# A hand-planned order of 3311 steps, planned anew for the attention part, with eight cross-engine waits in place of ten

## The chip, the core and the metric

The kernel runs on one core of a Trainium2 chip. Five engines work side by side, each through its own instructions in the order in which they were issued: TensorE (PE), VectorE (DVE), ScalarE (ACT), GpSimd (POOL) and SyncE (SP), which only starts DMAs here. The metric is the device time of one execution in microseconds.

## The reference

A local causal attention with a memory term, then two mixture-style feed-forward blocks one after the other on the same tokens:

```python
scores = (q @ k.T) / sqrt(64), causal          # 4 batches, 8 heads, 576 tokens, 64 wide
local = softmax(scores) @ v
q_p = phi(q)                                   # phi(x) = x + 1 for x > 0, else exp(x)
mem_out = (q_p @ M_prev) / (q_p . z_prev + 1e-6)
x = g * mem_out + (1 - g) * local              # g = sigmoid(beta) of the head
x = x as 2304 tokens x 512
x = mish(x @ w_in) @ w_out                     # 512 -> 2048 -> 512
x = silu(x @ w2_in) @ w2_out                   # 512 -> 2048 -> 512
```

## The kernel before

**Steps.** The kernel does not schedule itself. It registers 3311 named steps (`Steps.add`), each a Python function that issues one or a few instructions of one engine, and `Steps.issue` calls them in the order of a table, `ORDER`, which is a base64 string of step numbers. The tile library then puts semaphores where tiles are shared. So the table fixes the order on every engine's queue, that of the DMA issues on SP among them, and also which of a ring's buffers a step gets.

**The attention** works on 16 pairs of heads, numbered 0 to 15; a step is written "pair.step" below. ld.. loads qT, kT, nq and nv (L353). phu, phe (ACT, L385, L386), phn, phf, phz, phy (POOL, L388 to L394) and phr (DVE) make phi(q) and its product with z. The scores s0 to s41 are PE matmuls (L473, L508); r.. (DVE, L466) scale them, mask them and take the row minimum; e.. (ACT, L491) are the exponentials. zd, phq, zg, phmh, phml, phm0 are the scale factors and the scaled phi (DVE and POOL). X1, X2, X3 and W are transposes on PE (L366) that are copied out of PSUM by ACT and DVE (L356, L359; the step names end in Ah and Bh). Rw and Rl send the row scales through DRAM and back into a tile R (L448, L453, L455). Vhi and Vlo are the products with v (L565), and Vhic and Vloc (DVE, L569) multiply them by R and write the tokens into xT.

**The feed-forward blocks** (the MoE part) run 24 visits, each a group of four weight blocks on a third of the tokens. A product Q:vc/n (visit v, half c, product n, L881 to L883) is six matmuls into PSUM; s1, s6, s5 (ACT, L910) copy partial sums out, c11, c22, c21 (DVE, L908) add to them, m.. (ACT) are the activation functions, and h0, l0, h1, l1 split the result in a high and a low part (ACT L919, DVE L920). O:vc/.. are the six-matmul pieces of the second matrix (L948). The tokens are split once per third (0, 1, 2) by casts h.. (ACT, L853) and subtractions T.. and l.. (DVE, L846); sp.. (SP, L860) spills such a tile to DRAM. Weights are decoded in steps W:job/ld, abs, b0, b1, b2, b3 (DVE, L687 to L702) and hi (ACT, L723), lo (POOL L728 for the first four jobs, DVE for the others), and combined in steps C (L747).

**The manual waits.** `AFTER` is a list of pairs of step numbers: the second step's first POOL instruction waits for the first step's last DVE instruction, which is always a weight decoding step.

```python
for first, second in AFTER:
    if n == second:
        one, two = (next(i for i in x if i.engine == e) for x, e in (
            (reversed(of[first]), tc.nc.vector.engine), (of[second], tc.nc.gpsimd.engine)))
        tc.add_manual_dep(two, one.name, ...reason="no port shared")
```

Of the kernel before, what the change touches and what calls it, by code (L numbers as in the profile page):

```python
# [1130 lines left out]
ORDER = (
    "BQAGAEMABwBEAC4AKQBCABcAKgAAAAEAKwACAC8ALAADAIAAMAAcABoABAAYAG8KGwAdAB8ACQASAEYACwAKAAgAEQAtAEcADABIABMAgQAZABUA"
    "ZgANABQAawBZAB4AaQAOAGcASQAWAL4AbAAPAFQAIABaAGgASwBwChAAagB/ADEAXABbAEoAJAAyAFcAbQCDACEAVQC9ADQAWAAzAHEKNQBOACMA"
    "JQAmAEUANwBMACIATwA2AFYAhQA9AF0AvABSADgAPgBQAJYAhAA/APkAqABTAIYAowCZAFEAlwCpADsAOgCRAHUKqgCIAKYAhwCYAKQAXgCUADkA"
    "wACSAGEATQClAG4Acgo8AIsAbwBiAGAAcQCMAJoAcwBjACcAlQA2AXQAjwCnAHIAjQDCAHAA+wCJAMEAdQBfAHMKwwDOAHYAdwCOAPoA4AAoAHoA"
    "0QCQAEAAxAB8AHsAzwCTAHgAigB0CuUAxQDSAIIA0wCrAEEA0ACbAOYA4wBkAOEAOAGcAKwAdgquAC8M1gCxANQA/QCtAJ0AsADXAHkAtwDGAK8A"
    "5wDVAMgA/wB1AbkA/gDJALIAuADKAMcA5AAAAbUAzABzAbMACwHiALQAzQAQAXcKAgE3AQwBngA6AQEBfQBlAKAADgHLALYAEwF4Cp8AIgHoAB0B"
    "FAF+AL8AoQDpAHkKPAHrAA0BHgHqABEB7gB7Cg8BIwEgAe0AAwEkAfQA7AAhAQUBBAH2APUABgEfAaIA7wA7AbABCQHYAPAAPQHxAE0B2QAHAboA"
    "dAEKAVABPwEIAU4BegryANsAsgFRAbsASAF3AXwK3QAwDFoBeQESAV8BSwH3AE8BJQFgAfMAXQHcAFsBPgFJAUwBsQEYAdoAXAFDARoBJgF9CkIB"
    "KAFhAUAB7wFKATIM3gBGAV4BKwG0AUQBKQGBCkcBKgH4AJwBJwHfABkBMQyXAUUBMQGaAZgBFQEyATMBQQHuATMMhQF4ARcBFgEsAZ0BegFiAYgB"  # L1140
    "LwGeAfwAigGGAZkBUgEtAWMBiwFlAYcBfAGNAWYBVAGbAYABZwEwAVMBLgF/AXsBjgFVAYMBiQFpAYEBVgFkAcIBLAK2AX4KfQHUAWoB2QGEAYIK"
    "GwF+AcUBKwJoAYwB1wE0DMMBggFrATUMOQHEAccB1QGfATYMHAHxAW4BoAFXAcYB7QGiATQB2gGkAcoBbwHIAaMBOAxwAaUBkgHWAYMKoQG8AbUB"
    "bAEqAjUBOgy9AdsBlAGrAcABkwHLAbcBZwK+AY8BwQERAq0BFgLJAf8BkQG4AW0B2AEUAqwBFwKmARICdgG5AQICGAIEAvMBvwG6AVgBAwIHAqkB"
    "aQIFArsBpwHcAYQK8gEAAi4CcQGFCggC3QGqAYYK3wEGAvoBqAGQAd4BhwrgAfkBcgEBAlkB4QHPATAC/QGVAeIB0AH0AdEBNwz7AbMBFQJ/Ci8C"
    "9QHjAf4BEwKWAWgCQQLkAeUBTgJEAlMC9gFCAugBMQL8AaYCVAJPAjwC6gHpAVECQwLMATICGQL3AUUCrgHmAaQCPwLNAfgBPQI8DDMCUAIJAhoC"
    "pQKvAWsCHAIbAs4BNwIfAgoCNgJtAgsCQALwAQwCOgJVAiUCDQI0Ah4CPgJ5AucBHQInAjsC6wE5DDgCJgJ6AjkCIwLjAjUCfAKLAiACUgKICoAK"
    "fgIOAnsCiQqQAlYC0gF9AowCJAJXAoECWQIhAlgCjgJaAqgCfwKPCpECXAIiAmwCdAJbAqoC7AFiAm4C0wGSAnMCZAJjAkYCggJ3AnACYAJJAuEC"
    "jQJvAkgCSgK7AngCdQJdAj4MLQJLAqkCtgK+Aj8MRwJxAigCvwJhArwCcgJ2AqsCuQLiAo8CzQK3AsgCugIpAg8CrAJeAl8CIAOAAssCyQK9Aq0C"
    "zgKKCsoCkwKQCrACHgM7DIsKhgLMApQCsQIQArgClgJMApgCagK0AogClwKHArIC5QKZAq4CQAwfA+YC+AJNApUCtQLnAvMC+wJdA7MC+QKfAvYC"
    "rwLPAj0MmgKgAqECBQP8AtACCgP0Ap0CZQJbA/oC0QIIA9ICmwIGA9MCjArWAgcDgwILA40KZgLUAu4CnAKeAoQC6ALtAoUCCQPDAgwDpwLvAtwC"  # L1150
    "xAKRCukCNQPdAt4C9wKiAjYD2gJcAyIDOAPqAvEC1QIkA0cDQQzFAkIDIwOjAtcC9QKSCiUDMAPbAtkC2ALrAsACOQOaA4kCkwpCDMEC8gJDAzMD"
    "lwrwAuwCMQMmA98CRAOKAl8DRQMNAw4DNANIA8ICDwMAA+QCJwNEDBADKgPgAhMDKAMCAysDRgw3AxkDLAMBA8YCGgMbAxEDLQOUChIDFwOZA0YD"
    "LgMyA4QDKQOYCmEDfwNgA8cCmAP9AoIDLwOAAxQD/wJJA20DYgOFAxgDgwMWAxUDcgNKA24D/gKfCjoDmQqcA2QDAwNLA3UDYwOGA3ADbwNzA54D"
    "mgohA00DZQNxA0wDaANQAzsDPANnA08DQwwEA1YDTgNpA3YDZgNRA50DRQxrA6oDgQNYA1IDrwOfA1MDVwMcA6sDdANUA60DagOhA6ADsgPBA2wD"
    "XgOwA7wDHQM9A7EDmwpZA64DwgNVAz8DswO/A4cDvQN3Az4DnArAA6QDiAO+A6IDpwqlA4oDwwONA0ADrAOoA44KeAOmA6kDWgOJA4wDpwN5A5MD"
    "mwOjA0EDiwPEA5QDlQN6A8UDfAOgCo4DkQPHA3sDxgPKA5ADjwO0A8gD0AO1A7YDyQPRA9IDywPVA6gKFwR9A84DzQOSA8wDGAQdBBMEGgS3A88D"
    "0wOhCrgDFAS5A5YDJgSpCh4EIAS6AxsEFQQcBNQDoQQjBCcEtQQkBKgElQqqCqIEfgOWCigEuwOXA6MEqwTWAyEEMASkBK8EqwqpBLgEFgS8BBkE"
    "MQQpBLYEMgSsCqUEvwQ0BCoEtwSqBDMEKwSmBL0ErQTDBCwErQq5BKwEogotBLEEpwS+BKMKrwo7BOIErgSkCrAEugQ8BLMEJQThBMEEnQq0BMAE"
    "5ASeCrIE6ARIBLsE6wT1BCIEwgQ1BMQE9gQuBMcEyQSwCjkESQTMBB8EpQo6BEUEpgr4BMgExQTPBO8ExgTjBC8EtwpGBNAE6QT8BDYEygT/BD4E"
    "NwTNBEsEOATLBPcETATRBM4EsQrSBP0EQQTVBEIEPQTlBLgKuQq6CtgE6gS7CrIK2QSzCrwK5gRDBL0K+QTsBD8EVATWBLQKUQTtBMMK/gTTBLUK"  # L1160
    "AQUDBVIE+gTXBPEEvgrbBFMEtgpVBNwErgrECucE3QS/Ck4E3gRABO4EAAXACvAETwQkBdQE8gQhBUQEIgVWBCgF8wT7BAUF9AQjBVcExQrGCtoE"
    "AgXfBFAExwoEBVgEOAXgBAcFwQoJBSkFyAoIBTUFyQoGBSUFPAU3BSoFLQUmBT0FJwXKCssKOQXMCkcMwgosBSsFDAVIDM8KSgwvBUkMPgUPBUsM"
    "TAwQBUoETQxODGEFQQVQDDEFNgUyBToFPwVoBc0KOwUNBVMMQgXOChEFCgVSDFQM1woOBVYMEgVVDAsFVwzQChMFLgVYDDAFFQVZDEMFWgzRClsM"
    "YgUYBdIKXAxPDGMFMwVRDNMK2AoWBdQK2QrfCmQF2goXBTQFFAUbBWsFaQVdDEQFWQQeBWUF4AocBeEKagVHBeIKHwVABUgFHQV2BUUF4wpvBdsK"
    "GQXkCkYFZgXnChoFIAVeDEkF3Ap4BXUF7wPoCkwFfAV/BXcFbQXpCk8F6gp9BU0EbAVKBWcFSwV5BUcETQV+BXEFgQVSBesKTgVuBXoFcgVwBeAD"
    "7Ap7BYAFcwWhBYIFUwXXA1UFVAWoBVgFWQXvClAFWgVbBd0DVgWjBVcFgwWEBV4F+wOkBdUKhQXWCqIFXwWrBYYFrwXsA7UF3Qp0BakFXAWHBfAK"
    "UQXxCqUF8grtCogFYAXaA4kFqgXeCrwF7gqMBfMKpgX0CrcF9QqNBb0FrAW4BbEF+wpdBbkF5QrhBb4F8APBBbYFsgX2CroF6AWtBb8FjwX3CuED"
    "+Ar8CooF+QqOBZAF+gr9CqcFiwUBC+MFrgWwBbsFswWSBfwDtAWVBeYK6QXABcIF4gX+Cv8K5QUCC+QF6gWWBe0FAAvnBQMLBwvrBeYF7wXuBQQL"
# [137 lines left out]
```

## Time and profile before

| what | value |
|---|---|
| median of three runs | 924.39 us (923.96 to 924.99) |
| the profiled execution | 924.26 us, of which the span from the first to the last instruction is 922.5 |
| mean granted TensorE clock | 0.996 of full speed |
| busy share of the span | PE 99%, DVE 69%, ACT 50%, POOL 13% |
| attention on PE | from 4.81 us to about 159.9 us |
| first product of the feed-forward part on PE | 159.91 us |

The busy shares are averages over two stages: up to about 160 us the attention, in which DVE and ACT are as full as PE, and after that the feed-forward blocks, in which PE alone is full.

### The profile page before, as it was taken

The page shows a single profiled execution, that of the slowest core. Times are in us where ns is not written, and L with a number is a line of the kernel's source. Part 1 is how long each engine was busy: PE and PEld are TensorE (multiplying, and loading weights), DVE is VectorE, ACT ScalarE, POOL GpSimd, SP SyncE. Part 2 cuts the span into 40 slices and gives each one's busy share as a digit, 9 for nine tenths or more (in the row PEclk, how much of TensorE's full clock was granted, in tenths as well). Part 3 has the DMA queues.
Part 4 walks back from the last instruction along what each step waited for, and adds up shares of the span by engine and source line. Part 5 has one row for each costly group of instructions (what it writes and reads, how often), then busy time and mean ns, then how long its engine had stood idle before and what let it go on. Part 6 is the DMA issues. An engine that isn't in the chain of part 4 may idle for free.

```text
span 922.5 us, 15456 instructions
## 1 busy us (share of the span) xinstructions
...
## 2 busy tenths in 40 slices
...
GB/s 243 197 220 209 198 201 117 260 225 121 134 307 148 89 79 176 206 47 125 142 173 64 148 194 126 129 170 214 169 140 47 192 200 88 1 102 199 20 58 171
DMA packets 54794, 139.50 MB, mean 151 GB/s; under 512 B 7216, under 2 KB 26816, under 8 KB 54720
## 3 DMA queue, kind: packets, MB, share of 16 engines
...
q14 instruction: 27, 0.22, 0.1%
...
## 4 chain that ended last, share of the span: by engine, by line
PE 90%; DVE 3%; ACT 3%; DMA 1%; issue 1%; SPq 1%; POOL 0%; ACTq 0%; DVEq 0%; POOLq 0%
PE acc L948 44%; PE psX L881 7%; PE psX L883 7%; PE psX L882 7%; PE psY L881 4%; PE psY L883 4%; PE psY L882 4%; PE ps_t L565 3%; PE ps_s L473 3%; PE ps_t L366 2%; PE psW L883 2%; PE psW L881 2%; PE psW L882 2%; DVE sm L466 1%; ACT Ph L491 1%
## 5 line engine op out<-in xcount | busy, mean ns | idle before, releaser
L948 PE MATMUL acc<-g,w 128*128 128x384 f32 x1152 | 217.6, 338 | 0.0
L948 PE MATMUL acc<-w,g 128*128 128x512 f32 (+1 forms) x876 | 213.6, 392 | 0.0
L948 PEld LDWEIGHTS acc<-g,w 128*128 128x128 f32 x1152 | 203.9, 188 | 0.2 <-DVE g L920 0.2
L948 PEld LDWEIGHTS acc<-w,g 128*128 128x128 f32 x876 | 162.2, 188 | 31.7
L910 ACT COPY vt<-psX 128x384 f32<-128x384 f32 x144 | 67.8, 479 | 189.0 <-PE psX L883 158.3
L973 DVE TENSOR_TENSOR xT<-acc,xT 128x384 f32<-128x384 f32 (+2 forms) x127 | 75.8, 607 | 83.3 <-PE acc L948 83.2
L920 DVE TENSOR_TENSOR g<-vt,g 128x768 fp32r<-128x768 f32 x96 | 91.7, 965 | 37.8 <-ACT g L919 37.7
L908 DVE TENSOR_TENSOR vt<-psY,vt 128x384 f32<-128x384 f32 x96 | 52.8, 554 | 70.7 <-ACT vt L910 41.3
L919 ACT CAST g<-vt 128x768 fp32r<-128x768 f32 x96 | 78.7, 834 | 26.4 <-PE acc L948 25.5
L466 DVE CUSTOM_DVE_ANT_0 sm<-ps_s,mask 128x448 f32<-128x448 f32 (+3 forms) x128 | 66.6, 551 | 11.4 <-PE ps_s L473 7.5
L916 ACT ACTIVATE vt<-vt 128x768 f32<-128x768 f32 x48 | 40.3, 845 | 54.9 <-DVE vt L908 54.7
L881 PE MATMUL psX<-x,w 128*128 128x384 f32 x192 | 64.9, 338 | 0.4 <-ACT vt L910 0.4
L473 PE MATMUL ps_s<-kT,qT 64*128 64x288 f32 (+3 forms) x320 | 61.2, 474 | 3.7 <-DVE m L466 3.3
L881 PE MATMUL psY<-xT,w 128*128 128x384 f32 x192 | 64.7, 337 | 0.0
L883 PE MATMUL psY<-xT,w 128*128 128x384 f32 x192 | 64.7, 337 | 0.0
L883 PE MATMUL psX<-x,w 128*128 128x384 f32 x192 | 64.7, 337 | 0.0
L882 PE MATMUL psY<-xT,w 128*128 128x384 f32 x192 | 64.7, 337 | 0.0
L882 PE MATMUL psX<-x,w 128*128 128x384 f32 x192 | 64.7, 337 | 0.0
L756 ACT CAST w<-val 128x512 fp32r<-128x512 f32 (+1 forms) x64 | 35.3, 566 | 44.6 <-DVE val L747 20.7
L747 DVE TENSOR_TENSOR w<-val,w 128x512 fp32r<-128x512 f32 (+1 forms) x56 | 34.3, 620 | 23.7 <-ACT w L756 23.6
L491 ACT ACTIVATE Ph<-sm,m 128x448 f32<-128x448 f32 (+1 forms) x64 | 46.1, 724 | 0.3 <-DVE m L466 0.2
L914 ACT ACTIVATE vt<-vt 128x384 f32<-128x384 f32 x48 | 25.3, 526 | 40.6 <-DVE vt L908 40.6
(128 smaller groups left out, 1661.5 us busy)
## 6 DMA issues: line engine op xcount, KB each, us to landing
...
x<-sp SPq DMA_DIRECT2D x18, 768.0 KB, 6.2
sp<-x SPq DMA_DIRECT2D x12, 768.0 KB, 6.6
xT<-sp01T SPq DMA_DIRECT2D x9, 768.0 KB, 4.2
xT<-sp11T SPq DMA_DIRECT2D x9, 768.0 KB, 7.8
...
```

Source lines behind the costliest of these rows:

```text
L466: nc.vector.tensor_tensor_reduce(out, ps, mask, -0.125, init, ALU.add, ALU.min, acc)
L473: nc.tensor.matmul(ps, lhsT=s["qT"][R[j], qcols(i)], rhs=s["kT"][R[j], k0 + cols.start:k0 + cols.stop], start=True, stop=True)
L491: nc.scalar.activation(ptile(i)[:, o:o + w] if i else G("P0")[:, 1], s[f"sm{i}{j}"], AF.Exp, bias=s[f"m{i}"][:, j:j + 1], scale=-1.0, accu ...
L881: nc.tensor.matmul(o, lhsT=W(0, kc), rhs=X(0, kc), start=(n in (1, 2, 7) and kc == 0), stop=False, skip_group_check=True)
L882: nc.tensor.matmul(o, lhsT=W(0, kc), rhs=X(1, kc), start=False, stop=False, skip_group_check=True)
L883: nc.tensor.matmul(o, lhsT=W(1, kc), rhs=X(0, kc), start=False, stop=(kc == 1), skip_group_check=True)
L908: nc.vector.tensor_tensor(o, self.bank[q, to], o, op=ALU.add)
L910: f[f"s{n}"] = lambda n=n: nc.scalar.copy(val(*at[n]), self.bank[q, "X"])
L919: f[f"h{c}"] = lambda c=c: nc.scalar.copy(hi(c), val(c))
L920: f[f"l{c}"] = lambda c=c: nc.vector.tensor_tensor(self.gt(q, c)[:, 1, :], val(c), hi(c).bitcast(F32), op=ALU.subtract)
L948: nc.tensor.matmul(y, lhsT=a, rhs=b, start=(c == 0 and k == 0), stop=(c == 1 and k == 5))
L973: nc.vector.tensor_tensor(part, acc, part, op=ALU.add)
```

## The change

The tables are replaced; no instruction, tile or size changes. Of `AFTER`, two entries go: 8.phz no longer waits for the b2 step of weight block 2 (in), and the lo step of weight block 1 (out) on POOL no longer waits for the b1 step of block 4 (out). The other eight entries stand as they were. In `ORDER`, the places from the first to about the 1530th step differ, and eight places near the 2170th.

```diff
-AFTER = ((2673, 53), (2675, 195), (2679, 257), (2687, 501), (2705, 745), (2706, 805), (2707, 3138), (2708, 786), (2712, 865), (2730, 2710))
+AFTER = ((2673, 53), (2675, 195), (2679, 257), (2705, 745), (2706, 805), (2707, 3138), (2708, 786), (2712, 865))
 ORDER = (
-    "BQAGAEMABwBEAC4AKQBCABcAKgAAAAEAKwACAC8ALAADAIAAMAAcABoABAAYAG8KGwAdAB8ACQASAEYACwAKAAgAEQAtAEcADABIABMAgQAZABUA"
...
+    "BgAFAEIABwBEACkALgAIABcALAAAAC8AAQAtAAIAKgADADAAQwArABwAGgAJABgARgBvCgsAHQAKAB8ASAASAAwABACAABEAHgAOAA0AGwCBABUA"
...
```

What that does is seen on the engines' queues. On ACT at the start of the program stand, before (Pl, P and Ph are exponentials of pair 0, bt and g the four gate copies, u, e and nq the phi steps of pairs 0 and 1):

```order
L324 ACTIVATE bt_86<-bt_86 128x8
L491 ACTIVATE Pl,zz_107<-sm,m_149 128x192
L491 ACTIVATE P_166,zz_107<-sm,m_157 128x64
L340 COPY bt_91<-btg 128x4x8
L344 COPY bt_91<-btg 64x4 x2
L340 COPY g_92<-g1c 128x4x8
L344 COPY g_92<-g1c 64x4 x2
L491 ACTIVATE Ph,zz_107<-sm,m_172 128x448
L385 ACTIVATE u_103<-nq 128x9x64
L385 ACTIVATE u_104<-nq 128x9x64
L386 ACTIVATE e<-u_103 128x576
```

and now:

```order
L324 ACTIVATE bt_86<-bt_86 128x8
L491 ACTIVATE Pl,zz_107<-sm,m_149 128x192
L491 ACTIVATE P_164,zz_107<-sm,m_153 128x64
L491 ACTIVATE Pl,zz_107<-sm,m_149 128x192
L385 ACTIVATE u_103<-nq 128x9x64
L385 ACTIVATE u_104<-nq 128x9x64
L386 ACTIVATE e<-u_103 128x576
L387 ACTIVATE nq<-nq 128x576
L340 COPY bt_91<-btg 128x4x8
L344 COPY bt_91<-btg 64x4 x2
L340 COPY g_92<-g1c 128x4x8
L344 COPY g_92<-g1c 64x4 x2
```

The two phu steps, which need the nq tiles from DRAM, moved ahead of the gate copies.

On ACT where the attention has ended and the first products run stand, before (vt<-psX are s1, then s6 and Q:01/s1, then s5 and Q:01/s6; xT_3315 is hT4 of the first third of the tokens, x_3311, x_3312 and x_3313 are casts of the second third):

```order
L853 CAST x0T_3165<-xT 128x768
L910 COPY vt<-psX 128x384
L723 CAST w_3276<-val 128x512
L853 CAST x_3311<-xT 128x768
L914 ACT_TABLE_LOAD
L914 ACTIVATE vt<-vt 128x384
L910 COPY vt<-psX 128x384 x2
L853 CAST xT_3315<-xT 128x768
L853 CAST x_3312<-xT 128x768
L853 CAST x_3313<-xT 128x768
L910 COPY vt<-psX 128x384 x2
L914 ACTIVATE vt<-vt 128x384
```

and now (xT_3323 is hT4, x_3321 and x_3319 are casts of the second third, the L910 rows are s1, s6, Q:01/s1, and s5 with Q:01/s6):

```order
L853 CAST x0T_3164<-xT 128x768
L910 COPY vt<-psX 128x384
L853 CAST xT_3165<-xT 128x768
L910 COPY vt<-psX 128x384
L853 CAST xT_3163<-xT 128x768
L853 CAST x_3321<-xT 128x768
L910 COPY vt<-psX 128x384
L853 CAST x_3319<-xT 128x768
L853 CAST xT_3323<-xT 128x768
L910 COPY vt<-psX 128x384 x2
L914 ACT_TABLE_LOAD
L914 ACTIVATE vt<-vt 128x384
```

No cast of the second third stands any more between hT4 and the pair with s5, where two stood, and the table load moved behind that pair. On PE the products that begin there were Q:00/1, Q:01/1, Q:00/2, Q:00/6, Q:00/7, Q:01/7, Q:01/2, Q:00/5, Q:01/6, Q:00/3 and are now Q:00/1, Q:01/1, Q:00/6, Q:00/2, Q:00/7, Q:01/7, Q:00/5, Q:01/6, Q:00/3.

On SP at the same place stand, before (rd and R are the row scales of pairs 14 and 15, sp the first spill):

```order
L448 DMA rd_3076<-h_3035 9x128
L448 DMA rd_3181<-h_3126 9x128
L453 DMA R<-rd_3076 64x512
L455 DMA R<-rd_3076 64x64
L453 DMA R<-rd_3076 64x512
L455 DMA R<-rd_3076 64x64
L453 DMA R<-rd_3181 64x512
L455 DMA R<-rd_3181 64x64
L453 DMA R<-rd_3181 64x512
L455 DMA R<-rd_3181 64x64
L860 DMA sp_3254<-x_3162 128x1536
```

and now:

```order
L448 DMA rd_3181<-h_3125 9x128
L860 DMA sp_3187<-x_3160 128x1536
L453 DMA R<-rd_3071 64x512
L455 DMA R<-rd_3071 64x64
L453 DMA R<-rd_3071 64x512
L455 DMA R<-rd_3071 64x64
L453 DMA R<-rd_3181 64x512
L455 DMA R<-rd_3181 64x64
L453 DMA R<-rd_3181 64x512
L455 DMA R<-rd_3181 64x64
L860 DMA sp_3263<-x_3161 128x1536
```

The spill of the split tile x11 now stands ahead of all eight loads of R for the last two pairs.

## Rows read from the trace of the kernel before

**Rows 1.** Windows: stretch, length, busy us of each engine, clock, DMA share, GB/s

```profile
6.80:10.20 3.40, 2.89 (x10) 0.86 (x6) 2.57 (x12) 2.91 (x13) 0.88 (x4) 1.00 1.03 405
...
23.00:140.00 117.00, 114.87 (x1528) 81.81 (x1528) 113.38 (x372) 116.07 (x332) 90.73 (x141) 1.00 0.63 202
...
190.00:905.00 715.00, 715.00 (x3808) 678.66 (x3807) 454.20 (x805) 289.47 (x513) 0.00 (x0) 1.00 0.39 137
```

**Rows 2.** Waits of PE, 0 to 190 us: total, times, longest

```profile
PE psX L881 <- ACT vt L910: 0.4, 1, 0.4
```

**Rows 3.** Waits of ACT, 10 to 147 us

```profile
ACT h L356 <- DMA R<-rd: 0.2, 1, 0.2
ACT Ph L491 <- DVE m L466: 0.2, 1, 0.2
```

**Rows 4.** Waits of ACT, 147 to 160 us

```profile
ACT h L356 <- PE ps_t L366: 1.0, 4, 0.3
```

**Rows 5.** Timeline of ACT, 6 to 13 us: start, us, instruction, idle before

```profile
8.21 0.22 ACT L340 COPY bt<-btg 128x32 f32<-128x32 f32 x1 [0.35 <-POOL btg L335]
...
9.96 1.24 ACT L385 ACTIVATE u<-nq 128x576 f32<-128x576 f32 x2
...
12.69 0.67 ACT L387 ACTIVATE nq<-nq 128x576 f32<-128x576 f32 x1
```

**Rows 6.** Tile nq, 0 to 10 us: its loads, and their time to landing

```profile
L353 SPq DMA_DIRECT2D nq<-in_q_dram x3: 328/432/441, 1.6 to 7.2; - x3
...
DMA to landing us min/median/max: 6.5/6.5/6.5
```

**Rows 7.** Timeline of PE, 159 to 187 us

```profile
159.91 0.45 PE L881 MATMUL psX<-x,w 128*128 128x384 f32 x1
...
169.98 0.44 PE L881 MATMUL psX<-x,w 128*128 128x384 f32 x1 [0.43 <-ACT vt L910]
...
185.91 1.69 PE L948 MATMUL acc<-g,w 128*128 128x384 f32 x8
```

**Rows 8.** Timeline of DVE, 152 to 188 us: the first row is l11

```profile
153.59 0.95 DVE L846 TENSOR_TENSOR x<-xT,x 128x768 fp32r<-128x768 f32 x1
...
160.79 0.49 DVE L569 TENSOR_TENSOR xT<-ps_t,R 128x320 f32<-128x320 f32 x1 [0.65 <-DMA R<-rd]
...
162.06 0.95 DVE L846 TENSOR_TENSOR x0T<-xT,x0T 128x768 fp32r<-128x768 f32 x1
162.93 0.42 DVE L697 TENSOR_SCALAR val<-val 128x512 uint32<-128x512 uint32 x1
...
165.66 0.68 DVE L699 SCALAR_TENSOR_TENSOR val<-stg,val 128x512 uint32<-128x512 uint32 x1
```

**Rows 9.** Timeline of ACT, 158 to 185 us

```profile
163.01 1.28 ACT L914 ACT_TABLE_LOAD   x1
...
167.99 1.56 ACT L853 CAST x<-xT 128x768 fp32r<-128x768 f32 x2
169.46 0.85 ACT L910 COPY vt<-psX 128x384 f32<-128x384 f32 x2
```

**Rows 10.** Timeline of DVE, 181 to 188 us: l1 and l0 of Q:01 in one row

```profile
183.12 2.92 DVE L920 TENSOR_TENSOR g<-vt,g 128x768 fp32r<-128x768 f32 x2
```

**Rows 11.** Timeline of POOL, 145 to 190 us: the lo steps of blocks 1 and 3

```profile
163.49 1.29 POOL L728 TENSOR_TENSOR w<-val,w 128x512 fp32r<-128x512 f32 x1 [11.56 <-DVE val L697]
...
182.61 1.76 POOL L728 TENSOR_TENSOR w<-val,w 128x512 fp32r<-128x512 f32 x1 [3.28 <-ACT w L723]
```

**Rows 12.** Timeline of DVE, 119 to 126 us: a b2 step during a phf

```profile
123.52 0.91 DVE L699 SCALAR_TENSOR_TENSOR val<-stg,val 128x512 uint32<-128x512 uint32 x1
```

**Rows 13.** Timeline of SP, 152 to 164 us: the first load of R of pair 14

```profile
153.17 0.45 SPq L453 DMA_DIRECT2D R<-rd  x1
```

**Rows 14.** DMA issues: count, KB each, median us from issue to landing

```profile
sp<-x SPq DMA_DIRECT2D x12, 768.0 KB, 6.6
...
R<-rd SPq DMA_DIRECT2D x32, 128.0 KB, 3.2
```

More of the change, by code (lines that the diff above doesn't have):

```diff
@@ L1129 @@
 PERIOD = 7.5
-AFTER = ((2673, 53), (2675, 195), (2679, 257), (2687, 501), (2705, 745), (2706, 805), (2707, 3138), (2708, 786), (2712, 865), (2730, 2710))
+AFTER = ((2673, 53), (2675, 195), (2679, 257), (2705, 745), (2706, 805), (2707, 3138), (2708, 786), (2712, 865))
 ORDER = (
-    "BQAGAEMABwBEAC4AKQBCABcAKgAAAAEAKwACAC8ALAADAIAAMAAcABoABAAYAG8KGwAdAB8ACQASAEYACwAKAAgAEQAtAEcADABIABMAgQAZABUA"
[L1133 to L1168, printed above, removed]
@@ new lines @@
+    "BgAFAEIABwBEACkALgAIABcALAAAAC8AAQAtAAIAKgADADAAQwArABwAGgAJABgARgBvCgsAHQAKAB8ASAASAAwABACAABEAHgAOAA0AGwCBABUA"
+    "RwATABkAawBJAGYADwAWAL0AWQBpABQAZwBLAGwASgAgAH8AVABcAGoAMQBaAGgAEAAyAG0AvgAzAF0ANAAkAFcANgBbAFUAIQAmAHAK+wBYAEwA"
+    "TgBxCiMAgwA1AE8AvAAlADcAIgBWAIUAPQBQAIQAUgA+AJYAhgA/AKgAUwCjAJkAOwA4APoAlwBRAE0AhwCpAKYAkQCYADoAqgCkAF4AOQCSAKUA"
+    "PACUAGEAwABuAIwAbwBgAJUARQBxAIsAcACIAGMAmgBzACcAjQCnAHIAdQpfAI8AdABiAHIKwgCJAHUAjgAoAM4A+QBzCsEAdwDTAJAAwwB6ANEA"
+    "kwA2AUAA1AB2AM8AxAB7AKsA1gDSAHwA5QCbAIoA/QB2CngArACCAOAAdAqcAK0AZADQAOMAxQBBAK4A5ADmADgBsQDhANcAnQCvAOcAdwq3ALAA"
@@ new lines @@
+    "4gDGAC8MNwH/ALkAyADJAP4AuADMALIA1QDKALUAAAF5AAsBswC0AM0AEAFzAQ4BywACAccAngABAQwBEQF9AJ8AtgA6AegA6QB4CqAA6wATAR0B"
+    "ewoNAeoA7gAiAWUAoQA8AewAHgEDARQB7QAgAR8BeQq/AA8BIwH0AH4AOwEGAfYA9QA9AXUBBQEkAaIAEgHvAAcB2ADwAD4BCQHyAE0BdAEIAfEA"
+    "ugDZAHoKCgFQAdsATgEhAfMAfApIATAM3QB3AbsA/ABaAU8BeQFfAUsBUQH3AGABSQHcALIBYQFdATIMWwFMASUBGAHaAAQBPwFeAUMBJgF9ClwB"
+    "KAFCAbABSgErAd4ARgEpARoBGQFEASoBgQpHAUABJwExDEUBnAH4AJcB3wB4ATEBYgEzDJgB7wG0AZoBFQEzAUEBMgGFAXoBnQEXARYBLAGeAbEB"
+    "hgG2AYoBewGIAZkBUgGNAZsBLwGLAS0BfAFjAS4BfwGHASwCZQFmAYABVAFTAWcBVQGMAYMBZAFpAYkBMAE0DIEBwgFWAWgBfQGEATkBxwHFAX4B"
@@ new lines @@
+    "agEbATUMwwGOAe0BggqCAYMKawG1AdkBfgruAfEBtwHUAVcBbgHGAZ8B2gHKATQBbwEqAqAB1QGiARwB2wGkAdcB1gHIAbkBxAGSAXABowG9AZMB"
+    "hAqlAbwBlAFsATUByQGPAaEBwAFnAjYM2AGrAb4BywG4ARYCEQKsAZEB/wFtAb8BFALzARcCEgKmATgMrQErAgQCwQG6AToMcQEYAgACkAGpAXYB"
+    "BQIVArsBBwI3DFgBhQoIAtwBAgLyAaoB3QGGCi4C3wH6AagBpwFoAuEB+QETAnIB4AHPAQMCWQGVAf0B3gHQAaUC4gEBAn8K9AEwAvsBaQIGAtEB"
+    "4wH+AZYBQQL2AeUB9QEvAk4CUwKHCkQC/AFCAugBUQIxAjwC5AFPAhkC9wHpAcwBQwJUArMB6gH4Aa4BRQIaAj8CzQEcAh8CPQJQAuYBpgIbAgkC"
+    "awLOAR0CNwJAAh4CrwE2AgsCMwIKAqQCMgIMAj4COAIlAg0COgJ5AiYCbQLnAScCUgKLAjsCfAKQAiMC4wLrATkMNAJVAjkCegI1AjwMjAIgAuEC"
@@ new lines @@
+    "DgJWApECiAo+DH4CbAIiAtIBqAJXAokK8AFZApICfwJYAn0C7AFcAo4CWgIhAoECJAKNAmICWwLTAY8CgApuAnMCqgJ0AmQCYwJGAnUCewJgAkkC"
+    "jwp3AoICcAK7Am8CRwJLArYCqQK8Ar4CdgJdAqsC4gJIAsgCeALNAl8CDwLJAl4CrAItAnECygLOAoACuQKtAr0CcgJhApMCKAKQCj8MSgK3AjsM"
+    "IAPLAroClAKKCoYClgIQAr8CsAKVAosKQAyxAuUCHgMpAkwCiAKyArgCmQK0ApgCzAJdAz0MhwKuArMC+AJNArUC8wKXAh8D+QKvAvsCzwLnAp8C"
+    "5gL2ApoCoAKhAgUD+gJBDNACCgP0AmUCagL8AtECCwMIA9MCmwKMCtYCDAMGAyIDgwJcA50CnALoAu0CJANmAu4ChQKEAqcCwwLSAvcC1ALcAsQC"
+    "1QLvAjUDCQNbA+oC3QKRCqIC8ALeAukCxQIHA9oCngLXAjYD8QIjA5IKMAM4A9gCJQPZAvUCQgPAAjMD8gLbAkcDkwonA4kCwQINA+sCNAOXCkIM"
```

19 lines of the change are left out of this document (18 added, 1 removed).

## Prediction

> **What bounds the kernel now.** I read the windows first [rows 1]. From 190 to 905 us PE is busy 715.0 of 715 us, so nothing before that point can come back later: PE's work there is fixed, and the end moves by exactly as much as PE reaches it earlier or later. The change touches the orders before about 190 us and leaves PE's instructions the same, so the question is what PE loses up to there. In the attention from 23 to 140 us three engines are full at once: ACT 116.07 of 117 us, PE 114.87, DVE 113.38 [rows 1]. PE's figure holds stalls inside its pipelined groups, so it is not a floor; ACT's is the work itself, and it has 0.93 us to spare. The waits of ACT say the same from the other side: two waits of 0.2 us each between 10 and 147 us [rows 3]. Thus the attention is bound by ACT, whose work does not change. Only then do the waits of PE matter: after 10 us or so the one I can price in the feed-forward part is 0.4 us for ACT's copy of a partial sum [rows 2], at 169.98 us on the timeline, in front of Q:00/3 [rows 7].
>
> **The change part by part.** It removes no instruction. So I go along ACT and PE, and ask at each place where the order differs who is late now.
>
> *Head of ACT.* Before, the gate copies (8.21 us, after 0.35 us of waiting for POOL) ran ahead of the two phu steps at 9.96 [rows 5]. Now one more exponential and the two phu stand ahead. The first nq is issued at 1.6 us and lands 6.5 us later, at 8.1 [rows 6]; the second is 384 KB behind it, 0.95 us at the 405 GB/s of that stretch [rows 1], so about 9.1. The first phu can run at about 8.2 and end at 8.85 (half of the 1.24 us row [rows 5]), and ACT then waits about 0.25 us for the second nq. Phu, phe, phn and the copies follow without a wait and end at about 12.0. Before, the same work but for an exponential and a phe more and a phn less (0.67 + 0.57 - 0.58 = 0.66 us; an estimate: the phe and the phn as a phu from start to start, the exponential as the whole phn row [rows 5]) was done at 12.69 [rows 5]. 12.69 - 0.66 is 12.03. Term: 0.0; bounds -0.35 (the wait for POOL is spared and nothing replaces it) and +0.5 (the second nq lands 0.5 later than I think).
>
> *Middle of the attention.* The order lists show the same work ahead of the last exponentials and the last copies of pairs 14 and 15 on ACT and DVE, before and after; in between steps trade places with near neighbours. A step that is moved later, such as 9.X2Ah, holds a PSUM buffer longer, but which buffer the next step gets is decided by the same order, and the next steps get others. Term: 0.0. Below, the two waits of [rows 3] go: -0.4. Above, there is no row for it; DVE's own slack there, 117 - 113.38 = 3.6 us [rows 1], is what a new misfit would use up first, and I take +1.3, about one long GpSimd step, as the bound.
>
> *The dropped wait of 8.phz.* POOL no longer stands still for b2 of weight block 2, and this b2 step is now issued on DVE while 8.phf is likely to run. What such an overlap costs shows at 123.52 us: a b2 step took 0.91 us during a phf [rows 12] where one alone took 0.68 [rows 8], so +0.23 us on DVE, which its slack covers. Term: 0.0. The Trainium skill (SBUF — State Buffer, section "SBUF: two separate sides") says that DVE and GpSimd hold their shared port pair as an exclusive lock for a whole instruction, so that the loser fully blocks. By that rule this b2 step could stand for a whole phf; the sum would then be as in the third rival below. The second dropped wait binds nothing: POOL's lo of block 1 waits for ACT's hi step, which now comes after the b1 step that it waited for.
>
> *Tail of the attention.* PE's steps from 15.s41 on are the same ones, with 14.Vlo and 15.Vlo exchanged, and ahead of 15.X2Bh on DVE stand as many splits (three of 0.95 us) and short decoding steps (one) as before. So Q:00/1 stays at 159.91 [rows 7]. ACT's four waits there sum to 1.0 us [rows 4]; they are waits for PE, and removing them is the lower bound, -1.0.
>
> *The first products.* The third product is now Q:00/6, which needs lT2. In the row before, lT2 ends at 162.06 + 0.95 = 163.01 [rows 8]. From ahead of it go the wait of 0.65 for R, 15.Vloc and lT3 (the two 1.27 from 160.79 to 162.06); in their place come one short decoding step (about 0.4) and a b2 step (0.68) [rows 8]: 163.01 - 1.92 + 1.08 = 162.17. Nine products lie between 159.91 and 169.98 - 0.43, so one takes 1.07 us [rows 7] and the third is due at 162.05. Term: +0.1; bounds 0 and +0.5. Then the copy s5: before, two casts of the second third (1.56 us from 167.99) kept ACT until 169.46 [rows 9], and PE waited for it. Now they stand elsewhere; Q:00/5, as the seventh product, ends at about 167.6, s5 follows at once and is done by 168.1, and Q:00/3, as the ninth, is due at 168.6. Term: -0.4; bound 0.
>
> *The table load and the third lo step.* Before, the 1.28 us load at 163.01 lay in a gap of ACT [rows 9]. Now it stands behind s5 and Q:01/s6, at about 168.9, ahead of the activations. ACT also gets one more cast ahead of the hi step of block 3 and Q:01/h0; I count both about 1 us later than before, h0 ready at about 184.1. The lo step of block 3 on POOL starts then, too. Before, this lo took 1.76 us and l1 with l0 on DVE 2.92 us in one row [rows 10, 11]; a lo alone took 1.29 [rows 11] and a pair of such subtractions 1.9 (2 x 0.95, [rows 8]), so the meeting cost DVE 1.0 us. O:01/20 stands behind as many steps as before and is due at 185.91 + 0.1 - 0.4 = 185.6 [rows 7]. It wants l0 about 0.2 us and l1 about 0.7 us after its start. Without a meeting l1 ends at about 185.9, in time; with one at 186.9, 0.6 late. Term: +0.3, half of it; bounds 0 and +1.1.
>
> *Sum.* 0.0 + 0.0 + 0.0 + 0.1 - 0.4 + 0.3 = 0.0 us against the profiled execution's 924.26 us (span 922.5 and 1.76 around it), which lies 0.13 under the median of 924.39. **I predict 924.3 us.** A measurement of this kernel can tell about 0.2%, 1.85 us, from no change, that is outside about 922.5 to 926.2.
>
> **The rivals.**
>
> *Faster, because ACT's leftovers go.* If the new order fits the chip's durations better, ACT loses its wait for POOL at the head (0.35), the two in the middle (0.4) and the four in the tail (1.0), and PE the 0.4 in front of Q:00/3: 924.26 - 2.15 = 922.1 us. For it speaks that all these waits sit on engines that are full. Against it: the waits add up to just over the 1.85 us, so nearly all of them must vanish, with no new one.
>
> *Slower, because R comes late.* The spill of x11 stands ahead of the loads of R. It waits for l11, which ran from 153.59 to 154.54 [rows 8], so the first load of R moves from 153.17 [rows 13] to about 154.95, and the 768 KB go ahead of it in the queues; a spill takes 6.6 us to land by the median, a load of R 3.2 [rows 14]. Before, the last R was there at 160.79, when 15.Vloc could start [rows 8]; now at 162.5 if only the issue shifts, and up to 166 if the loads queue behind a spill that ends at 161.5 and more. 15.Vhic wants it at about 163.5, behind it on DVE stand T4 and lT1, and lT1 is wanted by Q:00/5 with about 0.1 us to spare. Each us beyond 163.5 costs PE one. It decides from about 165.4; at 166.0 the time is 924.3 + 2.5 = 926.8 us. Against it: R is small, and the issue alone leaves 1 us of room.
>
> *The port lock bites in the attention.* DVE's b2 step stands for the rest of a phf, about 1.2 us at the worst, and this reaches ACT because DVE is nearly full: 924.3 + 1.2 = 925.5 us. Against it: the 0.23 us above. It is the Trainium skill's rule on the shared port pair (SBUF — State Buffer) that would make it so; l1 and l0 at 183.12 agree with the rule, the b2 step at 123.52 paid less.
>
> **How the numbers follow.** My sum 0.56; the port lock 0.10, still within the bound of 0.2%; faster as in the first rival 0.18; slower by late R, or by the meeting at 184 us together with it, 0.16. Hence faster by over 0.2% 0.18, within 0.66, slower 0.16. The range reaches to the faster rival's 922.1 and to late R's 926.8, leaving about a tenth on either side: 922.2 to 926.6. The likeliest case alone spans 923.3 to 925.5.
>
> **What would show it.** Right: ACT busy about 116 of 117 us between 23 and 140; Q:00/1 within 1 us of 159.9; no wait in front of Q:00/3, at most 0.3 in front of Q:00/6; the first phu at about 8.2; a lo step on POOL that lies across l0 or l1 near 184, and a wait of PE there below 1 us. Wrong: Q:00/1 earlier or later by over 1.5 us, which would mean that the attention is not held by ACT's work; a wait of DVE at Vhic or Vloc for R after 163 us; new waits of ACT in the attention that sum to more than 1 us.

## The result, and the profile after

The changed kernel takes 929.76 us (median of four runs, 928.71 to 930.56) against 924.17 us for the kernel before beside it, 5.6 us more. The ratio on record is 1.0054, with a 95% interval of 1.0040 to 1.0069; it is not the quotient of the two medians, which is 1.0060 and lies inside the interval. The profiled execution took 928.71 us with a span of 926.9, so the traces differ by 4.4 us of span.

Weight blocks are written W:pbm below: feed-forward block p (0 the first, 1 the second), weight block b, matrix m (0 in, 1 out); W:020 is block 2 (in) of the first. C:01 are the combining steps of its second pair of weight blocks. Windows of the changed kernel, columns as in [rows 1]; the row 194.40:909.40 is cut 4.4 us later than its counterpart there, and PE is as full in it to 0.3 us:

```profile
23.00:140.00 117.00, 113.16 (x1500) 79.50 (x1496) 114.21 (x365) 113.18 (x324) 88.88 (x137) 1.00 0.64 203
194.40:909.40 715.00, 714.68 (x3804) 677.79 (x3803) 454.53 (x805) 290.81 (x515) 0.00 (x0) 1.00 0.39 135
80.00:140.00 60.00, 58.03 (x768) 40.80 (x764) 59.46 (x180) 56.97 (x160) 48.07 (x72) 1.00 0.65 205
```

The same window of the kernel before, a part of the stretch 23:140 of [rows 1]:

```profile
80.00:140.00 60.00, 59.90 (x808) 42.79 (x806) 58.54 (x186) 59.25 (x167) 49.02 (x76) 1.00 0.62 200
```

The loss is there. ACT is busy 56.97 of 60 us where it was busy 59.25, and PE does 768 matmuls where it did 808. DVE goes the other way: busy 59.46 instead of 58.54, with fewer instructions (180 for 186). An engine that is busier while it gets less done has instructions that take longer. DVE's timeline at three places, and POOL's at the same places:

```profile
83.08 1.87 DVE L699 SCALAR_TENSOR_TENSOR val<-stg,val 128x512 uint32<-128x512 uint32 x1
84.88 0.74 DVE L466 CUSTOM_DVE_ANT_0 sm<-ps_s,mask 128x576 f32<-128x576 f32 x1
...
100.53 1.91 DVE L702 SCALAR_TENSOR_TENSOR val<-stg,val 128x512 uint32<-128x512 uint32 x1
102.36 0.68 DVE L359 COPY h<-ps_t 128x512 f32<-128x512 f32 x1
...
137.52 1.51 DVE L697 TENSOR_SCALAR val<-val 128x512 uint32<-128x512 uint32 x1
```

```profile
82.99 1.42 POOL L390 TENSOR_TENSOR e<-e,nq 128x576 f32<-128x576 f32 x1
...
100.49 1.40 POOL L390 TENSOR_TENSOR e<-e,nq 128x576 f32<-128x576 f32 x1
...
137.46 1.28 POOL L391 TENSOR_TENSOR u<-e,nq 128x512 f32<-128x512 f32 x1
```

The reader should subtract ends. The phf step on POOL ends at 82.99 + 1.42 = 84.41, and the decoding step W:020/b2, which started 0.09 us behind it and alone takes 0.68 [rows 8], ends at 83.08 + 1.87 = 84.95: 0.54 us after POOL let go. At the other two places it is 0.55 us (b3, alone 0.68) and 0.29 us (b1, alone 0.42). So a decoding step that starts just behind a GpSimd step is held until that step has ended; the profile counts the held time as busy. By the Trainium skill (SBUF — State Buffer, "SBUF: two separate sides") the port pair that the two engines share is an exclusive lock: of a VectorE instruction that needs it and a GpSimd instruction, the one that starts first has it for the whole instruction, and the other blocks. These rows agree.

Eight decoding steps are held in this way by more than 0.1 us before 160 us. Their usual length is 0.42 us (abs, b0, b1) or 0.68 (b2, b3), and what they took beyond it sums to 5.3 us, where the kernel before has 0.34:

| held step | by | time held, us | places in ORDER before (step, holder) | places now |
|---|---|---|---|---|
| W:010/b0 | 2.phml | 0.37 | 234, 205 | 208, 210 |
| W:020/b2 | 8.phf | 1.19 | 545, 539 | 540, 541 |
| W:001/abs | C:01/l2 | 0.45 | 629, 681 | 634, 635 |
| W:020/b3 | 10.phf | 1.22 | 630, 660 | 661, 662 |
| W:011/abs | C:01/S1 | 0.14 | 719, 687 | 710, 711 |
| W:001/b2 | C:01/S3 | 0.52 | 723, 742 | 726, 727 |
| W:011/b0 | 11.phml | 0.36 | 800, 814 | 806, 799 |
| W:021/b1 | 14.phz | 1.09 | 925, 919 | 918, 919 |

In the new order the GpSimd step stands directly behind the decoding step in six of the eight pairs, in the seventh two places behind, in W:011/b0 seven ahead; none of the eight pairs has an entry in AFTER. Standing behind in the table does not mean running behind: POOL was free and got there first, by 0.04 to 0.14 us in seven of the pairs and by 0.46 us in that of W:011/abs.

PE feels it through the steps queued behind the held one. Between 80 and 160 us the kernel before has no wait of PE that the profile lists. The changed kernel has two, and they follow W:020/b2 and W:020/b3; the view of its waits there, and the two on its timeline:

```profile
PE ps_t L366 <- DVE h L359: 1.0, 1, 1.0
PE ps_s L473 <- DVE m L466: 0.7, 1, 0.7
```

```profile
87.90 1.02 PE L473 MATMUL ps_s<-kT,qT 64*128 64x448 f32 x4 [0.71 <-DVE m L466]
...
103.10 0.58 PE L366 MATMUL ps_t<-ident,Ph 64*128 64x64 f32 x11 [1.04 <-DVE h L359]
```

The row at 87.90 waits for a mask step that DVE ends at 87.84; DVE comes to it from the held b2 without a gap. The row at 103.10 waits for the copy at 102.36, queued behind the held b3. Together they are 1.7 us. The 40 missing matmuls are more than that, some 3 us at the rate of the kernel before (an estimate, 60 us x 40 / 808); the rest is not listed as a wait. Between 10 and 80 us PE's listed waits are 5.3 us in place of 3.9; 0.8 us of them, at 39 us, is for a copy of ACT's; it stays when no step is held, and the last experiment comes back to it. ACT, which had waited 0.4 us between 10 and 147 us [rows 3], now waits 4.0 us (1.4, 1.2, 1.0 and two of 0.2) in the view of its waits up to 151, the first three rows of which are:

```profile
ACT h L356 <- PE ps_t L366: 1.4, 3, 0.7
ACT W L356 <- PE ps_t L366: 1.2, 3, 0.6
ACT Pl L491 <- DVE m L466: 1.0, 3, 0.6
```

The timeline of PE, to be read against [rows 7]: Q:00/1 comes 3.77 us late, O:01/20 (the third row here) 3.66, and then PE waits once more:

```profile
163.68 0.45 PE L881 MATMUL psX<-x,w 128*128 128x384 f32 x1
...
177.74 0.44 PE L881 MATMUL psY<-xT,w 128*128 128x384 f32 x1 [0.21 <-DVE vt L908]
...
189.57 2.47 PE L948 MATMUL acc<-g,w 128*128 128x384 f32 x12
...
201.87 0.44 PE L881 MATMUL psX<-x,w 128*128 128x384 f32 x1 [0.32 <-ACT vt L910]
```

So of 4.4 us, 3.8 are lost up to the end of the attention, nothing in the first 24 pieces of six matmuls of the MoE part, and 0.7 behind them: PE's pieces come 3.7 us late at 191 us and 4.4 from 204 us on.

### The profile page after: what moved, and what is told of

It is laid out like the page before. It is cut to its first block, busy times and chain, and to the rows that moved or that the text cites. A ratio compares the mean times of both kernels' runs of the same rounds, so it can differ in the third digit from the quotient of the medians.

```text
span 926.9 us, 15456 instructions
## 1 busy us (share of the span) xinstructions
PE 909.7 (98%) x5964; PEld 824.2 (89%) x5964; DVE 638.7 (69%) x1325; ACT 463.9 (50%) x975; POOL 119.8 (13%) x189
## 4 chain that ended last, share of the span: by engine, by line
PE 84%; DVE 6%; ACT 5%; DMA 2%; issue 2%; SPq 1%; DVEq 0%; ACTq 0%
PE acc L948 43%; PE psX L881 7%; PE psX L883 7%; PE psX L882 7%; PE psY L881 3%; PE psY L883 3%; PE psY L882 3%; DVE sm L466 2%; PE ps_t L565 2%; PE psW L883 2%; PE psW L881 2%; PE psW L882 2%; PE ps_s L473 2%; ACT Ph L491 2%; PE ps_t L366 1%
## 5 line engine op out<-in xcount | busy, mean ns | idle before, releaser
L948 PEld LDWEIGHTS acc<-w,g 128*128 128x128 f32 x876 | 162.2, 188 | 31.7
L910 ACT COPY vt<-psX 128x384 f32<-128x384 f32 x144 | 68.1, 480 | 188.8 <-PE psX L883 153.4
L473 PEld LDWEIGHTS ps_s<-kT,qT 64*128 64x128 f32 x320 | 30.1, 193 | 19.2 <-DVE m L466 6.8
```

What stands on the lines that cost most here:

```text
L473: nc.tensor.matmul(ps, lhsT=s["qT"][R[j], qcols(i)], rhs=s["kT"][R[j], k0 + cols.start:k0 + cols.stop], start=True, stop=True)
L910: f[f"s{n}"] = lambda n=n: nc.scalar.copy(val(*at[n]), self.bank[q, "X"])
L948: nc.tensor.matmul(y, lhsT=a, rhs=b, start=(c == 0 and k == 0), stop=(c == 1 and k == 5))
```

## The experiments

Theory A: the loss is the decoding steps held by GpSimd steps, because the pairs in AFTER were found for the old order and the new order has other neighbours. Theory B: the new order is longer by itself, whatever the decoding steps meet. Each kernel but the changed one, whose time is that of the result, was timed in five rounds beside the kernel before. "Held" is the sum, up to 160 us, of what decoding steps took beyond their usual length in the profiled execution.

| kernel | waits | held, us | Q:00/1 starts | median, us | ratio to before (95%) |
|---|---|---|---|---|---|
| before | 10 | 0.3 | 159.9 | 924.2 to 925.0 | 1 |
| changed | 8 | 5.3 | 163.7 | 929.76 | 1.0054 (1.0040 to 1.0069) |
| changed, no wait | 0 | 7.6 | 167.0 | 932.00 | 1.0071 (1.0057 to 1.0085) |
| changed, four reduces | 8 | 1.6 | 161.7 | 927.05 | 1.0029 (1.0019 to 1.0039) |
| changed, five waits more | 13 | 0.8 | 160.8 | 927.16 | 1.0030 (1.0019 to 1.0040) |
| changed, ten waits more | 18 | 0.1 | 160.5 | 926.32 | 1.0015 (1.0006 to 1.0023) |
| the last, a copy moved | 18 | 0.1 | 159.7 | 924.77 | 1.0002 (0.9993 to 1.0011) |
| before, eight waits | 8 | 0.3 | 159.9 | 925.67 | 1.0013 (1.0005 to 1.0022) |
| before, no 8.phz wait | 9 | 0.4 | 160.0 | 924.76 | 0.9999 (0.9990 to 1.0008) |
| before, no W:011/lo wait | 9 | 0.3 | 160.0 | 925.37 | 1.0011 (1.0002 to 1.0020) |
| before, no wait | 0 | 3.0 | 162.7 | 928.24 | 1.0036 (1.0024 to 1.0048) |
| attention of before | 10 | 0.3 | 161.1 | 925.81 | 1.0009 (1.0000 to 1.0018) |
| attention of after, 13 waits | 14 | 0.7 | 162.2 | 926.40 | 1.0019 (1.0010 to 1.0028) |
| attention of after, 18 waits | 19 | 0.1 | 163.3 | 926.48 | 1.0023 (1.0014 to 1.0031) |

**Five waits more.** The pairs W:020/b2 and 8.phf, W:020/b3 and 10.phf, W:021/b1 and 14.phz, W:001/b2 and C:01/S3, W:001/abs and C:01/l2:

```diff
-AFTER = (..., (2712, 865))
+AFTER = (..., (2712, 865), (2687, 500), (2688, 622), (2714, 867), (2699, 3136), (2696, 3134))
```

> The changed kernel with five waits more, at the places where its trace shows a weight decoding step on VectorE that lasts 0.45 to 1.22 us too long under a GpSimd step: 8.phf now waits for b2 of weight block 2 (in), 10.phf for its b3, 14.phz for b1 of block 2 (out), and two combining steps for abs and b2 of block 0 (out). Theory A (GpSimd gets ahead of the decoding step and blocks it for its whole length, the 3.8 us that the attention ends later come from that): most of the five overlong steps (4.5 us too much in all) are back at their own length, the attention ends 2.5 to 4 us earlier than in the changed kernel, 925 to 927 us. Theory B (the order itself is worse on ScalarE and TensorE: buffers held longer, more waits for transposes): waits on GpSimd change nothing there, 928.5 to 931 us.

It took 927.16 us, 2.6 less than the change: 0.2 above theory A's figures and far below theory B's. DVE's and POOL's timelines at the first of these places:

```profile
83.25 0.68 DVE L699 SCALAR_TENSOR_TENSOR val<-stg,val 128x512 uint32<-128x512 uint32 x1
```

```profile
84.08 1.42 POOL L390 TENSOR_TENSOR e<-e,nq 128x576 f32<-128x576 f32 x1 [0.88 <-DVE val L699]
```

POOL now waits 0.88 us, 8.phf starts 1.1 us later than in the change, and the decoding step takes its 0.68. PE has no listed wait left between 80 and 160 us, and the row that stood at 87.90 starts at 87.09. Theory A.

**Four reduces.** The same order and waits as in the change, but in place of four of the held steps VectorE does a reduce of the same tile. The kernel leaves out that part of the decoding of these weights:

```diff
+            if (job, n) in REDUCED:   # W:020/b2, W:020/b3, W:001/b2, W:021/b1
+                nc.vector.tensor_reduce(out=c[:, :1], in_=c, axis=AX.X, op=ALU.add)
-            if n == 0:
+            elif n == 0:
```

> The changed kernel, with four of the blocked decoding steps (b2 and b3 of block 2 (in), b2 of block 0 (out), b1 of block 2 (out)) replaced by a reduction of the same 128x512 tile on VectorE. Order, waits and number of instructions stay; these weights are then not decoded fully. A reduction of 585 elements (phr) is never overlong in either trace while GpSimd works. Theory A: the four steps last 0.6 to 0.7 us in place of 1.2 to 1.9, 4.0 us less on VectorE, and the time falls by 2 to 4 us to 925.5 to 928. Theory B: no difference over 0.5 us from the changed kernel, 929 to 930.5.

It took 927.05 us, within theory A's figures and as with five waits, though no instruction waits for another that did not before. The reduce on DVE, and the 8.phf that started 0.10 us ahead of it on POOL:

```profile
83.88 0.68 DVE L698 TENSOR_REDUCE val<-val 128x1 f32<-128x512 f32 x1
```

```profile
83.78 1.41 POOL L390 TENSOR_TENSOR e<-e,nq 128x576 f32<-128x576 f32 x1
```

The meeting is the same and nobody is held. So it is not the neighbourhood of the two steps, nor a semaphore, but what the decoding instruction reads and writes. The same page of the Trainium skill (section "Who interferes with whom") says that on trn2 a reduce never contends; the 0.68 us agrees.

**Before, with eight waits, and with none.**

```diff
-AFTER = (..., (2687, 501), ..., (2712, 865), (2730, 2710))
+AFTER = (..., (2712, 865))
```

> The kernel before with its own order, but the eight waits of the changed kernel: the two dropped waits alone. Theory A: 8.phz starts at once after 8.phf, at the moment at which b2 of block 2 (in) is about to start; if it gets ahead, b2 loses up to 1.2 us, in a stretch where VectorE has some slack: 924 to 925.5. The other dropped wait binds nothing. Theory B: the waits do not matter, 923.9 to 924.6.

```diff
+AFTER = ()
```

> The kernel before with its own order and no manual wait at all. Theory A: seven or eight more GpSimd steps of 0.6 to 1.4 us get ahead of decoding steps and block them; the trace shows overlong decoding steps that sum to 4 to 8 us, and the time is 926.5 to 931. Theory B (the order is what counts): below 925.5.

The old order loses 3.7 us without its ten waits (928.24 against 924.52 beside it) and 1.15 without the two that the change dropped. The first lies within theory A's figures, though its decoding steps are held 3.0 us and not the 4 to 8 expected; the second is 0.2 above them, and that the wait of W:011/lo binds nothing was wrong in this order, as its own run below shows. The ten waits are thus worth more than the two orders differ by when hardly a step is held in either (1.3 us).

**Ten waits more, and none, in the changed order.** The ten are the five above and W:010/b0 with 2.phml, W:011/abs with C:01/S1, W:021/b2 with 15.phy, W:001/b3 with 11.phm0, W:011/b2 with 13.phy.

```diff
+AFTER = (... the eight and the five ..., (2679, 176), (2704, 3135), (2715, 929), (2700, 726), (2707, 807))
```

> The changed order with eighteen waits: its eight, the five of the first of these runs, and five more in front of the GpSimd steps that stand just behind a decoding step in this order (2.phml, C:01/S1, 15.phy, 11.phm0, 13.phy). Theory A (a decoding step that starts a little behind a GpSimd step is held for that step's length): W:010/b0 goes from 0.79 to 0.42 us and W:011/abs and W:021/b2 stay at 0.42 and 0.68, the excess of all decoding steps in the first 175 us falls from 0.8 us with thirteen waits to under 0.5, and the time is 926.5 to 927.2 us, at or just under that of thirteen waits. Theory B (the order itself is longer, whatever the decoding steps meet): 927.2 us, no better than thirteen waits. A further one, that each wait costs GpSimd something that attention then wants: above 927.6 us.

> The changed order with none of the eight waits. If the eight waits that were kept have become idle in the new order, because their two steps stand 2 to 31 places apart there: 929.3 to 930.3 us, as the change itself, and the excess of the decoding steps stays near 5.3 us. If they still hold collisions off, as the ten do in the order of before (where leaving all out cost 3.7 us): 932 to 934 us, with an excess of 8 to 9 us. If waits cost GpSimd time that the end feels: under 929 us.

With ten more, 926.32 us, a little under theory A's figures, and hardly a step held: the ten show no cost of their own. With none, 932.0, as expected if the eight still hold collisions off: I had thought it possible that the eight kept waits had become idle in the new order, and they have not. What a wait keeps apart is also not only its own pair: W:021/b0, which no entry names, ran ahead of 14.phf in the change and met it here (DVE, then POOL):

```profile
137.76 1.62 DVE L695 TENSOR_SCALAR val<-val 128x512 f32<-128x512 f32 x1
```

```profile
137.68 1.41 POOL L390 TENSOR_TENSOR e<-e,nq 128x576 f32<-128x576 f32 x1 [2.84 <-ACT e L386]
```

From eighteen waits to none the held time grows by 7.5 us and Q:00/1 comes 6.4 later, 0.86 us for each microsecond held. That is a mean and no price of a single hold: from eighteen waits to the change it is 0.6, from the change to no wait 1.4, in the old order 1.0.

**The orders spliced.** After 1034 places both orders have issued the same steps, the attention but for its last few; there they can be cut and joined. In words, as the table is only numbers:

```diff
-ORDER = before
+ORDER = first 1034 places of before, rest of changed          # ten waits
...
-ORDER = changed
+ORDER = first 1034 places of changed, rest of before          # 13 or 18 waits, and that of W:011/lo
```

> The first 1034 places (all but the last of attention) in the order of before, the rest in the changed order, with the ten waits of before. Theory A (the loss lies where the decoding steps collide, in attention): 924.3 to 925.4 us, the time of before and at most the 0.6 us that the span of the changed kernel gained behind Q:00/1. Theory B, with the loss in the opening of the MoE part: 926.5 us or more.

> The first 1034 places in the changed order with its eight waits and five more, the rest in the order of before with its wait of W:011/lo. Theory A: the 0.9 us that is left in attention at the first product of Q:00 with thirteen waits, so 925.2 to 926.2 us. Theory B, that the changed order of attention is itself the longer one by more than that: 927 us and more, as with thirteen waits and the changed rest.

> The first 1034 places in the changed order with eighteen waits, the rest in the order of before with its wait of W:011/lo. Theory A (what the changed order of attention costs is its collisions): 924.4 to 925.6 us, that is before plus at most the 0.6 us by which Q:00/1 still came late with eighteen waits. Theory B (the changed order of attention is longer by itself): 926.4 us or more, as with thirteen waits in this splice.

925.81, 926.40 and 926.48 us. The first is 0.4 over theory A's figures and below theory B's, the second 0.2 over theory A's; the other two do not differ although one holds its decoding steps 0.6 us less, and the last falls to theory B. So behind the collisions 0.8 to 2.1 us are left over, more of it with the attention of the changed order (2.1 with eighteen waits) than with its other part (0.8); the parts do not add up, as both together with eighteen waits leave 1.3. (Where Q:00/1 starts in these three is not to be compared closely: the profiled execution of the first was already 1.1 us late at 31 us, in the same order as before, and that of the last took 927.5 us, 1.0 above its median.)

**The two dropped waits one by one.**

> The order of before without the wait of 8.phz for W:020/b2 alone. By the trace of the run that lacked two waits, there 8.phz started 0.12 us behind W:020/b2 and was itself held 0.43 us, while W:020/b2 took its usual 0.68: 924.8 to 925.2 us, no change. If this wait were the one that counts (theory of a pair by pair price): 926 us.

> The order of before without the wait of W:011/lo for W:041/b1 alone. By the same trace W:041/b1 is held 1.1 us and Q:00/3 comes 0.7 us late: 925.5 to 926.0 us, as without both. If nothing hangs on it: 925.0 us.

The wait of 8.phz is worth nothing in the old order: 924.76 us, ratio 0.9999. There 8.phz starts behind the b2 step and is held itself, 1.70 us instead of the 1.28 of L391 above, on an engine with time to spare (DVE, then POOL):

```profile
83.59 0.69 DVE L699 SCALAR_TENSOR_TENSOR val<-stg,val 128x512 uint32<-128x512 uint32 x1
```

```profile
83.71 1.70 POOL L391 TENSOR_TENSOR u<-e,nq 128x512 f32<-128x512 f32 x1
```

The wait of W:011/lo is worth 1.0 us (925.37 against 924.41): without it W:041/b1 starts 0.18 us behind the lo step, among the splits that the first products want, and PE's wait in front of Q:00/3 is 1.1 us in place of the 0.4 of [rows 2] (DVE, then POOL).

```profile
162.58 1.51 DVE L697 TENSOR_SCALAR val<-val 128x512 uint32<-128x512 uint32 x1
```

```profile
162.40 1.41 POOL L728 TENSOR_TENSOR w<-val,w 128x512 fp32r<-128x512 f32 x1 [10.40 <-ACT w L723]
```

**A copy moved.** With eighteen waits the timeline of PE still showed a wait that the kernel before does not have; ACT's timeline below it shows why. The copy 2.X3Ah at 38.84, for which PE waits, stands behind the cast C:00/h1 and the step 4.phe:

```profile
39.47 0.34 PE L366 MATMUL ps_t<-ident,Pl 64*128 64x64 f32 x3 [0.77 <-ACT h L356]
```

```profile
37.74 0.62 ACT L756 CAST w<-val 128x512 fp32r<-128x512 f32 x1
38.25 0.70 ACT L386 ACTIVATE e<-u 128x576 f32<-128x576 f32 x1
38.84 0.58 ACT L356 COPY h<-ps_t 128x512 f32<-128x512 f32 x1
```

```diff
-... C:00/h1, 5.ldqT, 4.phn, 2.X3Bh, 3.s40, 3.s41, 4.phe, 2.X3Ah, 3.r41 ...
+... 5.ldqT, 4.phn, 2.X3Bh, 3.s40, 3.s41, 2.X3Ah, C:00/h1, 4.phe, 3.r41 ...
```

> The changed order with eighteen waits, and in it one step of ScalarE's moved: the copy 2.X3Ah stands ahead of the cast C:00/h1 and of the step 4.phe (0.5 and 0.6 us of slots between them) instead of behind them. With eighteen waits TensorE waited 0.77 us for that copy at 39.5 us, a wait that the order of before does not have. Theory B (what eighteen waits leave over, some 1.3 us against before, is in the order of steps on ScalarE and VectorE): that wait falls below 0.2 us and the time by 0.4 to 0.8 us, to 925.5 to 926.0 us. Rival: ScalarE is full there, the next copy or exponential is late instead, and the time stays at 926.3 us.

It took 924.77 us, 0.2 under the kernel before beside it (924.95), which is no difference. The wait is gone, and another of 0.49 us for DVE's mask step stands at 39.61 in its place, as one of 0.47 does at 39.55 in the kernel before; from 50 us on the steps of PE in the attention run 0.4 to 0.8 us earlier than with eighteen waits. That the order on ScalarE costs time here is what theory B said. The time fell by more than it said and than the trace shows (1.5 us between the medians, from two jobs; the two intervals overlap), so how much this one copy is worth is not settled.

## Why the prediction was wrong

I predicted 924.3 us with a range of 922.2 to 926.6; it is 929.76, above the range. To slower by over 0.2% I had given 0.16, and none of that to what happened: the port lock in the attention had 0.10, as a case that stays within 0.2%.

**The step that failed** is the one on the dropped wait of 8.phz, and with it the term for the middle of the attention. I wrote that an overlap of a b2 step with a phf costs "+0.23 us on DVE, which its slack covers", from the 0.91 us at 123.52 us [rows 12]. I knew that a phf was running, and did not hold the ends of the two rows against each other:

```profile
122.47 1.41 POOL L390 TENSOR_TENSOR e<-e,nq 128x576 f32<-128x576 f32 x1 [0.63 <-ACT e L386]
```

13.phf ended at 123.88. The b2 step met only its last 0.36 us, was held for that, and then took 0.55, as W:020/b2 took 0.54 once 8.phf had ended: the row is a full hold of a short rest, not a cheap overlap of a long step. It agreed with the lock and I took it as evidence against it. So the rival with the port lock was right in its mechanism, and its "Against it: the 0.23 us above" was wrong. Its size was wrong too: 1.2 us for one step, where eight steps are held 5.3 us in sum and Q:00/1 comes 3.8 us late. I priced the collision at the place where an entry of AFTER was deleted and did not look for the pairs that the new order made neighbours without any entry. The middle of the attention, 0.0 with a bound of +1.3, was most of the 3.8 us by which Q:00/1 is late: 3.2 of them are gone when hardly a step is held (160.5 with eighteen waits). Two of my own signs of being wrong were there: Q:00/1 late by over 1.5 us, and new waits of ACT of more than 1 us (4.0 in place of 0.4).

**ACT bounds the attention** held as a description of before, and failed as a reason for "no change": ACT is busy 113.18 of 117 us in the change, where I had named about 116 as the sign of being right. DVE's 3.6 us of slack in 117 [rows 1] lies in short gaps, the longest listed wait among them 0.5 us, and a hold of 1.2 us at one place is late for the mask step right behind it.

**The dropped waits themselves.** That 8.phz's costs nothing was right: in the change the step that holds W:020/b2 is 8.phf, 8.phz stands behind it, and in the old order this wait is worth nothing either. That the second one "binds nothing" was right for the new order: W:011/lo runs at 176.71 us there, and no step of DVE beside it takes more than 0.11 us too long. In the old order it is worth 1.0 us.

**Head of ACT.** Right. The two phu began at 8.52 us instead of about 8.2, and the instruction behind the gate copies started at 11.98, where I had them end at about 12.0:

```profile
8.52 1.35 ACT L385 ACTIVATE u<-nq 128x576 f32<-128x576 f32 x2
...
11.56 0.40 ACT L344 COPY g<-g1c 64x4 f32<-64x4 f32 x2
11.98 0.56 ACT L491 ACTIVATE Pl<-sm,m 128x320 f32<-128x320 f32 x1
```

**First products, table load, third lo step.** Their sum of 0.0 at O:01/20 came out at -0.1 (3.66 - 3.77). The wait of 0.4 us in front of Q:00/3 [rows 2] is gone, as forecast. In place of the +0.1 at Q:00/6 there is no wait, and one of 0.21 for c2 work on DVE at 177.74. The third lo step met l1 and l0, as forecast (1.86 us from 186.77 on POOL, 2.85 for the pair from 187.46 on DVE), but PE did not wait: the term of +0.3 was 0. Not forecast is the wait of 0.32 us at 201.87 for ACT's copy, part of the 0.7 us that are lost behind O:01/20; the rest of the 0.7 was not followed up.

**Late R** did not happen at the end of the attention. The first load of R was issued at 158.81 us:

```profile
158.36 0.35 SPq L860 DMA_DIRECT2D sp<-x  x1
158.81 0.47 SPq L453 DMA_DIRECT2D R<-rd  x1
```

That is the forecast 154.95 plus the 3.77 us by which all is late; the loads landed within 3.4 us, the spill did not delay them, and DVE has no wait for R after 140 us. Earlier it has: 1.0 us at 44.77 us and once 0.5 us after 80 us, where the kernel before has no wait for R on DVE ahead of the one at 160.79 us [rows 8]. With eighteen waits and the copy moved these waits are still 0.8 and 0.6 us while the time is that of the kernel before, so they do not carry the loss.

**What stays open.** The collisions explain what the waits gave back: the distance to the kernel before beside it falls from 5.6 to 1.3 us. With one order of three steps on ACT changed the rest is gone too, though the trace shows only 0.4 to 0.8 us for that. Why the two splices with the changed attention kept 1.4 to 2.1 us when nearly all holds were gone, was not settled; the same copy stands in both, and it was not moved there.
